# A second level of seven products in the gate and up products, and a deadline scheduler for units 2 to 27

## The chip, the core and the metric

The kernel runs on one core of a Trainium2 chip. The engines of that core are TensorE (PE, matrix products; its weight loads are shown as PEld), VectorE (DVE), ScalarE (ACT), GpSimd (POOL) and SyncE (SP); here POOL and SP only start DMA transfers, POOL those that add into DRAM or park a tile there, SP the plain loads and stores. Every engine works through its own instructions in the order in which the program lists them. The metric is the device time of one execution in microseconds (us), as a median over runs.

## What is computed

With x of 2048 rows and 512 columns, in fp32:

```python
xn = layernorm(x)                                # over the 512 columns
a, b = xn @ Wd_re.T, xn @ Wd_im.T                # DFT matrices, 512 x 512
A = Ws_re @ a - Ws_im @ b                        # DFT matrices, 2048 x 2048
g, u = xn @ w_gate, xn @ w_up                    # 512 x 1792 each
B = (gelu_tanh(g) * u) @ w_down                  # 1792 x 512
return x + A + B
```

## The kernel before

**Arithmetic.** An fp32 operand is split into a high part (`split_hi`, a copy on ACT that rounds to fp32r) and a low part (`split_lo`, a subtraction on DVE). `mm3` then makes one product of three matmuls: high by high, and high by low both ways. A matmul has 128 x 128 weights and 512 columns. All large products are done by a form of Strassen's algorithm with seven block products for a 2 x 2 block product (Winograd's form, with operands numbered 0 to 6), whose results are combined by copies between PSUM banks and by additions on DVE.

**Stages.** From 5 to 379.5 us the Fourier part runs (tiles `z`, `m`, `y`); its first two chunks are ordered by the planner below. From 379.5 to 771.3 us follow 28 units, and then the last down products.

**A unit.** `unit(n)` makes one 256-wide piece of the gate projection (n even) or of the up projection (n odd), for one half of the sequence: units 0 to 13 the first half, 14 to 27 the second (`NP` = 14; n // NP is the half `sp`). The weights are the same in both halves, unit n + 14 reads those of unit n again. A unit has seven products r, each over two blocks of 128 rows, so six matmuls each, in the order 0, 4, 5, 1, 6, 3, 2, in three PSUM banks `a`, `b`, `c`. Product 0 is the first: its result goes to bank `a` and is copied by ACT into bank `b` (line 1137), so that products 1 and 5, 6, 3 add to it in each. ACT copies `b` to the tile `q6` after product 5 and to `w` after product 6; DVE adds `c` to them. The four results go through gelu on ACT (`gate`, n even) or are multiplied in on DVE (`up_1`, n odd). Between the products stand "fills" (`fill`, up to four places per unit): pieces of the down product of earlier pairs (`down`), or, at first, the last Fourier products (`late_y`). The copies of a down product are added into DRAM (`partial`) by POOL's accumulating transfers.

**The work beside it.** `background(n)` lists, by hand, the DVE and ACT work of unit n: splits of the next unit's weights, sums of the weights of the unit after it (`weight_sums`), the same for the down weights `("d", q)`, the sums and splits of the hidden values of the pair before (`h_sum`, `h_split`), and the operands of x for the second half (`sums_xT`, `xT_split`), four of the seven of which are parked in DRAM (`PARKED`) and fetched again in units 11 to 13 (`FETCH`). `run(share)` issues a share of that list after certain products. `load_w(n + 2)` and `load_wd` start the weight loads one to two units ahead. In units 20, 21, 23 and 24 DVE finishes the output of the first half (`ends`, `finish`).

**Memory.** All tiles come from a pool of 109 slots of 128 x 512 (`SLOTS`); PSUM has eight banks.

**The planner.** `Plan` (line 37) is a list scheduler that runs when the program is built. `add` gives it an operation with its engine ("p" PE, "v" DVE, "a" ACT, "s" SP, "g" POOL), its price, what it comes after, which slots it makes and uses, and which banks. PE's operations stay in the order in which they are added. `deadlines` gives each PE operation the time at which it starts if PE never waits, and each other one the latest time that keeps those. `choose` picks the next operation on each engine: the earliest possible one, or one due sooner; it keeps the count of slots under a cap, starts an SP operation no sooner than `ahead` before it is due, and limits the transfers in flight. `run` then emits everything in the order found. Its prices are 0.6 us for a DVE and 0.52 for an ACT instruction of 512 columns (`V5`, `A5`) and 512/2400 + 0.0133 for a matmul (`MM`). Before the change it orders the first stage only, not the units.

**The tail.** `last_down` starts its first two banks in unit 27 and then works off the down products of the last two pairs.

Of the kernel before, what the change touches and what calls it, by code (L numbers as in the profile page):

```python
# [8 lines left out]
F32 = mybir.dt.float32  # L9
F32R = mybir.dt.float32r  # L10
# [4 lines left out]
P = 128  # L15
# [21 lines left out]
class Plan:  # L37
# [3 lines left out]
    LATE = 1e9  # L41
    LAND = .7

    def __init__(self, clocks, live, cap, ahead):
        self.clock, self.live, self.cap, self.ahead = dict(clocks), live, cap, ahead
        self.ops, self.users, self.ends, self.size = {}, {}, {}, {}
        self.products = None
        self.dma, self.flying = 0., {"s": [], "g": []}
        self.held, self.idle = {}, []
# [1 line left out]
    def done(self, name, at):  # L51
        self.ends[name] = at

    def add(self, name, engine, cost, fn, after=(), makes=(), uses=(), due=None, mb=0, banks=(), holds=(), adds=False):
        after = list(after)
        if engine == "p":
            if self.products:
                after.append(self.products)
            self.products = name
        self.ops[name] = dict(e=engine, cost=cost, fn=fn, after=after, makes=dict(makes), due=due, mb=mb, adds=adds, banks=tuple(banks), drains=bool(holds) and engine != "p")  # L60
        self.size.update(makes)
        for k in (*dict(makes), *uses):
            self.users.setdefault(k, set()).add(name)
        for k in (*banks, *holds):
            self.held.setdefault(k, set()).add(name)

    def deadlines(self):
        then = {n: [] for n in self.ops}
        for n, o in self.ops.items():
            for a in o["after"]:  # L70
                if a in self.ops:
                    then[a].append(n)
        t = self.clock["p"]
        for o in self.ops.values():
            if o["e"] == "p":
                o["due"], t = t, t + o["cost"]
        order, seen = [], set()

        def visit(n):
            stack = [(n, iter(then[n]))]  # L80
            seen.add(n)
            while stack:
                m, it = stack[-1]
                for c in it:
                    if c not in seen:
                        seen.add(c)
                        stack.append((c, iter(then[c])))
                        break
                else:
                    stack.pop()  # L90
                    order.append(m)
        for n in self.ops:
            if n not in seen:
                visit(n)
        for n in order:
            o = self.ops[n]
            own = self.LATE if o["due"] is None else o["due"]
            if o["due"] is None and o["drains"]:
                own = max([self.ops[a]["due"] + self.ops[a]["cost"] for a in o["after"] if a in self.ops and self.ops[a]["e"] == "p"],
                          default=self.LATE) + 4  # L100
            took = o["cost"] + (3.5 + o["mb"] * 2.6 if o["mb"] else 0)
            tail = self.TAIL[o["e"]]
            o["due"] = min([own] + [self.ops[c]["due"] - took - tail * (self.ops[c]["e"] != "p" or o["e"] != "p") for c in then[n]])
# [4 lines left out]
    def choose(self, ready, frees, spare):  # L108
        best = None
        for e, names in ready.items():  # L110
            able = []
            for n, at in names.items():
                o = self.ops[n]
                at = max(at, self.clock[e])
                if e == "s":
                    at = max(at, o["due"] - self.ahead)
                if o["mb"]:
                    k, room = self.parts(o), 8 if e == "s" else 7
                    for when, u in reversed(self.flying[e]):
                        k += u  # L120
                        if k > room:
                            at = max(at, when)
                            break
                if o["banks"]:
                    if len(self.idle) < len(o["banks"]):
                        continue
                    at = max([at] + self.idle[:len(o["banks"])])
                need = sum(o["makes"].values())
                if need:
                    cap = self.cap - (0 if o["due"] - at < 6 or not spare else 8 if e != "s" else 14)  # L130
                    live = self.live
                    for when, k in frees:
                        if when <= at:
                            live -= k
                        elif live + need > cap:
                            live -= k
                            at = when
                    if live + need > cap:
                        continue
                able.append((round(at, 1), o["due"], at, n))  # L140
            if not able:
                continue
            mine = min(able, key=lambda a: a[:2])
            until = mine[2] + self.ops[mine[3]]["cost"]
            for a in sorted(able, key=lambda a: a[1]):
                if a[2] < until - .1 and a[1] < min(mine[1] - 1, until):
                    mine = a
                    break
            if best is None or mine[2] < best[0]:
                best = mine[2], e, mine[3]  # L150
        return best

    def run(self):
# [3 lines left out]
        for n, o in self.ops.items():  # L157
            for a in o["after"]:
                if a in self.ops:
                    then[a].append(n)  # L160
        left = {k: len(u) + (len(u) == 1) for k, u in self.users.items()}
        of = {n: [] for n in self.ops}
        holding = {n: [] for n in self.ops}
        for k, u in self.held.items():
            for n in u:
                holding[n].append(k)
# [52 lines left out]
def fnet_geglu_kernel(ctx: ExitStack, tc: tile.TileContext, x, xt, cs, dh, wgu, wd, out):  # L219
# [16 lines left out]
    def slot(name, dtype=F32, shape=(P, D)):  # L236
        return mem.tile(list(shape), dtype, name=name, tag="mem")
# [4 lines left out]
    def hl_tile(name):  # L242

        return slot(name + "h", F32R), slot(name + "l", F32R)

    def hl_half(name):

        t = slot(name, F32R, (P, 2, HD))
        return t[:, 0], t[:, 1]

    def split_hi(t, src, sign=1):
        nc.scalar.activation(t[0], src, AF.Copy, scale=float(sign))  # L252
# [12 lines left out]
    def mm3(ps, a, sl, b, first, last, resumed=False, part=slice(3), late=0):  # L265

        for r, (u, v) in list(enumerate(((0, 0), (late, 1 - late), (1 - late, late))))[part]:
            nc.tensor.matmul(ps, a[u][:, sl], b[v], start=first and r == 0, stop=last and r == 2,  # L268
                             skip_group_check=resumed)
# [17 lines left out]
    def cols(j):  # L287
        return slice(j * P, (j + 1) * P)
# [9 lines left out]
    xnt = dram.tile([2, ND, P, CH], F32, name="xnt")  # L298
    d_park = dram.tile([7, 2, 2, P, 2, HD], F32, name="d_park")
    z_park = dram.tile([NC // 2, 2, 2, 2, P, CH], F32, name="z_park")  # L300


    xs, ln, xn = {}, {}, {}
# [377 lines left out]
    def flush():  # L681
        while pend:
            split_lo(*pend.pop(0))
# [158 lines left out]

    def weight_split(n, k):

        if k == 3:
            wl[n, 3] = hl_half("w")
            return wl[n, 3], wx[n][3][:, 0]
# [13 lines left out]
    def load_wd(q):  # L861

        if q < NP:
            wx["d", q] = [slot("wd", F32, (P, 2, HD)) for _ in range(2)]
            for i in range(2):
                nc.sync.dma_start(wx["d", q][i].rearrange("p a b -> p (a b)"), wd[q % (NP // 2), i])

    def product(n, k, ps, first=False):
        for i in range(2):
# [216 lines left out]
    def unit(n):  # L1086
# [48 lines left out]
        multiply(0, a, True)  # L1135
        q6, w = slot("q6"), slot("w")
        nc.scalar.activation(b, a, AF.Copy)
        multiply(4, c, True)
        while carry:
            carry.pop(0)()  # L1140
# [617 lines left out]
                y_out(c // 2, 3)  # L1758


    flush()
    add_w(1)
    carry.append(lambda: y_out(1, 6))
    for d in range(2):
        norm_xT(1, 0, d)
    last = last_down([NP - 2, NP - 1])
    for n in range(2 * NP):
        unit(n)
    for j in range(2):
        load_acc(1, 4, j)  # L1770
    for item in items:
        item()()
    next(last, None)


# [34 lines left out]
```

## Time and profile before

| | |
|---|---|
| median of 3 runs | 796.99 us (796.53 to 798.0) |
| the profiled execution | 796.45 us |
| its span | 794.7 us |
| PE busy, share of the span | 789.6 us, 99% |
| DVE, ACT, POOL busy | 718.9, 514.3, 162.0 us |
| moved by DMA | 179.58 MB |
| granted TensorE clock | 0.999 |

How to read it: a group of instructions is a line with the source line, the engine, the operation, output and inputs by the names of the tiles, count, busy time and mean length. Instructions of one engine overlap at their ends, so the mean length of one is longer than the distance between the starts of two. A chain piece or a timeline piece begins with its start and its length in us. The stretches list, for a window from one time to another, the busy us of PE, PEld, DVE, ACT and POOL, then PE's granted clock, the share of the DMA engines' time and GB/s. In this profile unit 0 begins at 379.54 us, unit 2 at 404.05, unit 4 at 431.34, unit 6 at 457.18, unit 14 at 571.42, unit 20 at 657.10, unit 26 at 742.78, and the tail at 771.34.

### The profile page before, as it was taken

What the parts mean: (1) busy time and instruction counts of PE and PEld (TensorE: products, weight loads), DVE (VectorE), ACT (ScalarE), POOL (GpSimd) and SP (SyncE); (2) the same over time, 40 slices, a digit from 0 to 9 for tenths busy, and PEclk for the clock granted to TensorE, in tenths of its full rate; (3) what the DMA queues carried; (4) which work ended last, traced back from release to release, by engine and by line L of the source; (5) the groups of instructions that cost most, each with busy time, mean ns of one, the idle gap of its engine ahead of it and who ended that gap; (6) DMA issues with size and microseconds to landing.
All of it is one profiled execution on the core that took longest, in us unless ns stands there. A gap on an engine that the chain in (4) does not pass through costs nothing.

```text
span 794.7 us, 11494 instructions
## 1 busy us (share of the span) xinstructions
PE 789.6 (99%) x3483; PEld 651.5 (82%) x3483; DVE 718.9 (90%) x1321; ACT 514.3 (65%) x982; POOL 162.0 (20%) x234
## 2 busy tenths in 40 slices
PE   9999999999999999999999999999999999999997
PEld 6888888888888888888888888888888888888886
DVE  7999999989999989899999998888878779989787
ACT  7997656547444655366667866766667676576663
POOL 0110420034211231000103422321222233122100
PEclk9999999999999999999999999999999999999999
DMA  9967997869999898779717977858975799887942
GB/s 340 364 174 228 344 350 258 269 242 243 365 372 363 296 304 292 254 263 308 169 55 162 218 144 164 203 90 213 263 142 86 124 252 140 181 203 140 256 95 106
DMA packets 94639, 179.58 MB, mean 226 GB/s; under 512 B 10960, under 2 KB 18672, under 8 KB 94384
## 3 DMA queue, kind: packets, MB, share of 16 engines
q1 hardware_dynamic: 68688, 118.80, 44.8%
q0 software_dynamic: 25600, 59.78, 35.4%
q8 instruction: 27, 0.44, 0.2%
q14 instruction: 36, 0.29, 0.1%
q10 hardware_dynamic: 288, 0.26, 0.1%
HBM read 116.13 MB, written 65.81 MB: 229 GB/s over the span
## 4 chain that ended last, share of the span: by engine, by line
PE 99%; DMA 0%; DVE 0%; ACT 0%; issue 0%
PE m L268 35%; PE dn L268 17%; PE b L268 14%; PE c L268 10%; PE y L268 10%; PE a L268 10%; PE z L268 4%; DMA x<-in_x 0%; DVE bn L332 0%; DVE p L1005 0%; DVE xa L355 0%; ACT w L343 0%; DVE stats L334 0%; PE st L1631 0%
## 5 line engine op out<-in xcount | busy, mean ns | idle before, releaser
L252 ACT ACTIVATE psh<-pan 128x512 fp32r<-128x512 f32 x203 | 115.6, 625 | 73.7 <-DVE pan L647 27.2
L257 DVE TENSOR_TENSOR psl<-pan,psh 128x512 fp32r<-128x512 f32 x198 | 128.5, 691 | 4.7 <-ACT psh L252 4.0
L926 POOL DMA_DIRECT2D partial<-part x94 | 80.8, 869 | 234.5 <-ACT part L925 200.3
L268 PE MATMUL m<-psh,xch 128*128 128x512 f32 x232 | 90.2, 389 | 0.0
L268 PE MATMUL m<-psl,xch 128*128 128x512 f32 x232 | 90.2, 389 | 0.0
L268 PE MATMUL m<-psh,xcl 128*128 128x512 f32 x232 | 90.2, 389 | 0.0
L925 ACT ACTIVATE part<-dn 128x512 f32<-128x512 f32 x94 | 55.4, 604 | 24.7 <-PE dn L268 22.4
L257 DVE TENSOR_TENSOR wl<-ws,wh 128x512 fp32r<-128x512 f32 x84 | 55.2, 685 | 0.1
L268 PEld LDWEIGHTS m<-psl,xch 128*128 128x128 f32 x232 | 43.5, 188 | 9.1
L268 PEld LDWEIGHTS m<-psh,xcl 128*128 128x128 f32 x232 | 43.5, 188 | 9.1
L268 PEld LDWEIGHTS m<-psh,xch 128*128 128x128 f32 x232 | 43.6, 188 | 9.0
L252 ACT ACTIVATE wh<-ws 128x512 fp32r<-128x512 f32 x84 | 49.6, 628 | 0.1
L1150 ACT ACTIVATE w<-b 128x512 f32<-128x512 f32 x28 | 16.7, 598 | 47.0 <-PE b L268 46.9
L568 POOL DMA_DIRECT2D partial<-part x28 | 20.9, 786 | 109.8 <-ACT part L564 104.0
L1153 DVE TENSOR_TENSOR w<-c,w 128x512 f32<-128x512 f32 x28 | 19.3, 690 | 24.5 <-ACT w L1150 24.5
L268 PE MATMUL m<-psh,xa 128*128 128x512 f32 x116 | 40.4, 389 | 0.0
L640 DVE TENSOR_TENSOR pan<-pan 128x512 f32<-128x512 f32 x58 | 38.2, 688 | 2.0 <-DMA pan<-in_cs 2.0
L257 DVE TENSOR_TENSOR htl<-s,hth 128x512 fp32r<-128x512 f32 x56 | 36.1, 688 | 4.2 <-ACT hth L252 4.1
L898 DVE TENSOR_TENSOR s<-s 128x512 f32<-128x512 f32 x56 | 37.5, 689 | 1.0
L257 DVE TENSOR_TENSOR wl<-wx,wh 128x512 fp32r<-128x512 f32 x28 | 19.2, 687 | 15.8 <-ACT wh L252 15.8
L252 ACT ACTIVATE hth<-s 128x512 fp32r<-128x512 f32 x56 | 32.4, 641 | 1.0 <-DVE s L898 1.0
L252 ACT ACTIVATE hh<-s 128x512 fp32r<-128x512 f32 x42 | 26.7, 635 | 9.4 <-DVE s L885 8.2
(774 smaller groups left out, 2338.6 us busy)
## 6 DMA issues: line engine op xcount, KB each, us to landing
pan<-in_cs SPq DMA_DIRECT2D x157, 256.0 KB, 5.4
partial<-part POOLq DMA_DIRECT2D x122, 256.0 KB, 5.4
wx<-in_wgu SPq DMA_DIRECT2D x56, 256.0 KB, 5.0
t_park<-pan POOLq DMA_DIRECT2D x29, 256.0 KB, 5.5
pan<-t_park SPq DMA_DIRECT2D x29, 256.0 KB, 4.8
wd<-in_wd SPq DMA_DIRECT2D x28, 256.0 KB, 4.3
acc<-partial SPq DMA_DIRECT2D x28, 256.0 KB, 5.8
zr<-z_park SPq DMA_DIRECT2D x16, 256.0 KB, 4.3
```

The lines of the kernel that those rows point to most:

```text
L252: nc.scalar.activation(t[0], src, AF.Copy, scale=float(sign))
L257: engine.tensor_sub(t[1], src, hi)
L268: nc.tensor.matmul(ps, a[u][:, sl], b[v], start=first and r == 0, stop=last and r == 2, skip_group_check=resumed)
L568: nc.gpsimd.dma_start(partial[sp, r, j], ypart.pop((r, j)), **({} if r in (0, 5, 6) else {"accum_op": OP.add}))
L640: return [lambda: nc.vector.tensor_sub(t3, b22, b12), lambda: nc.vector.tensor_sub(t1, b12, b11), lambda: (nc.vector.tensor_sub(b22, *((t1 ...
L898: nc.vector.tensor_sub(t, u, v)
L925: nc.scalar.activation(t, ps[j], AF.Copy)
L926: nc.gpsimd.dma_start(partial[sp, r, j], t, accum_op=OP.add)
L1150: nc.scalar.activation(w, b, AF.Copy)
L1153: nc.vector.tensor_add(w, c, w)
```

## The change

Two things change together.

First, units 2 to 27 are no longer run by `unit`. A new function `middle` gives all their work to a `Plan`: products in a written order, and everything on DVE, ACT, SP and POOL (weight loads, sums and splits, operands of x, copies out of banks, hidden values, down products with their accumulating transfers, the finishing of the first half, the loads of the last accumulators) by deadlines. `Plan` gets an argument `early`: an operation that makes tiles isn't started more than 16 us before it is due (`EARLY`), one that takes a bank not more than 3 us before; what has no deadline of its own is due just before PE's end. SP may load up to 16 us ahead (`FETCH_AHEAD`). Units 0 and 1 still run by hand.

Second, for the pairs of units 4 and 5, 6 and 7, to 12 and 13, product 0 is itself done by seven products, over the two units, the two row blocks and the two halves of the sequence (`inner_p`, `inner`). Each has one row block, so three matmuls. The operands of x for it are made once (`inner_x`), those of the weights once per pair (`inner_w`). The two results for the first half stay in PSUM: one in bank `a` of the even unit, one in bank `b2`, which serves as bank `a` of the odd unit. The two for the second half are parked in DRAM (`m_park`) and loaded again (`load_m`); units 18 to 27 (`fetched`) copy them into banks `b` and `a` in place of product 0, and need only half of their first weight split. The residual sums of x move to units 6 and 7 at the earliest, the x block (0, 1) is no longer parked and is split early, since the inner products use it.

Core of the diff:

```diff
+    LEAD = 4
+
+    def lead(n):
+        return n % 2 == 0 and LEAD <= n < NP
+
+    def fetched(n):
+        return isinstance(n, int) and n >= NP + LEAD
...
+    def inner(n, k, ps, first=False):
+
+        if k in (0, 1):
+            a, b = [t[:, cols(k)] for t in wl[n, 0]], xT[0, 0, k]
+        elif k == 3:
+            a, b = [t[:, cols(1)] for t in wl[n + 1, 0]], xi["hl", 3]
+        else:
+            a, b = [t[:, {4: 0, 5: 1, 6: 2, 2: 3}[k]] for t in wi["hl", n]], xi["hl", k] if k != 2 else xT[1, 0, 1]
+        mm3(ps, a, slice(P), b, first, True, resumed=not first)
...
+    U0, U1 = 2, 2 * NP
+    EARLY = 16
+    FETCH_AHEAD = 16
+    PARK = [(0, 0), *((k, i) for k in (1, 4, 5) for i in range(2))]
+
+    def middle():
+
+        plan = Plan(dict(p=.3, v=6.6, a=4.2, s=0., g=0.), 84, SLOTS - 2, FETCH_AHEAD, EARLY)
...
+        for n in range(LEAD, NP, 2):
+            for k in range(4):
+                add(("si", n, k), "v", .2, lambda n=n, k=k: inner_w(n, k), after=[("si", n, k - 1)] if k else [("lw", n), ("lw", n + 1)],
+                    uses=[("wx", n), ("wx", n + 1)] + [("wi", n)] * (k > 0), makes={} if k else {("wi", n): 1})
+            split_of(("iw", n), lambda n=n: inner_wsplit(n), [("si", n, 3)], [("wi", n)], {("wih", n): 2})
+            for j in range(2):
+                m = n + NP + j
+                add(("lm", m), "s", .45, lambda m=m: load_m(m), after=[("mp", m - NP)], mb=MB, makes={("m0", m): 1})
...
+            if lead(n):
+                b2, c2 = ("b2", n), ("c2", n)
+                inner_p(n, 0)
+                copy("ib", n, "b2", lambda n=n: bank_of(n, "a"), [("i", n, 0)], banks=[b2], holds=[a])
+                mult(n, 4)
+                inner_p(n, 1)
+                copy("sb", n, "b", lambda n=n: bank_of(n, "a"), [("i", n, 1)], banks=[b], holds=[a])
+            elif lead(n - 1):
+                copy("sb", n, "b", lambda n=n: bank[n - 1, "b2"], [("i", n - 1, 3)], banks=[b], holds=[a])
+                mult(n, 4)
+                inner_p(n - 1, 2)
+                sums("iaq", n - 1, "q2", "c2", [("i", n - 1, 2), ("iq", n - 1)], ("c2", n - 1))
+                add(("mp", n - 1), "g", .6, lambda n=n: nc.gpsimd.dma_start(m_park[n - 1], side[n - 1, "q2"]), after=[("iaq", n - 1)],
+                    uses=[("q2", n - 1)], mb=MB)
+            elif fetched(n):
+                copy("sb", n, "b", lambda n=n: m0[n], [("lm", n)], banks=[b], uses=[("m0", n)])
+                copy("sa", n, "a", lambda n=n: m0[n], [("lm", n)], banks=[a], uses=[("m0", n)])
+                mult(n, 4)
+            else:
+                mult(n, 0)
+                copy("sb", n, "b", lambda n=n: bank_of(n, "a"), [("p", n, 0)], banks=[b], holds=[a])
+                mult(n, 4)
+            d(0)
+            mult(n, 5)
+            copy("q6", n, "q6", lambda n=n: bank[n, "b"], [("p", n, 5)], holds=[b])
+            mult(n, 1)
+            hidden(n, (0, 0), [("p", n, 1)], lambda n=n: bank_of(n, "a"), [a], [])
+            d(1)
+            if lead(n):
+                inner_p(n, 4)
+            mult(n, 6)
...
+            if lead(n):
+                inner_p(n, 5)
+                copy("iq", n, "q2", lambda n=n: bank[n, "b2"], [("i", n, 5)], holds=[b2])
+            d(2)
+            mult(n, 3)
...
+            if lead(n):
+                inner_p(n, 6)
+                copy("iw", n, "w2", lambda n=n: bank[n, "b2"], [("i", n, 6)], holds=[b2])
+                sums("iaw", n, "w2", "c2", [("iw", n), ("i", n, 4)], c2)
...
+            d(3)
+            mult(n, 2)
...
+            if lead(n):
+                inner_p(n, 3)
...
     last = last_down([NP - 2, NP - 1])
-    for n in range(2 * NP):
+    for n in range(U0):
         unit(n)
-    for j in range(2):
-        load_acc(1, 4, j)
-    for item in items:
-        item()()
+    middle()
     next(last, None)
```

Here `mult(n, r)` is a product r of unit n, `inner_p(n, k)` an inner product k, `d(i)` the place of a fill, `copy` a copy on ACT and `sums` an addition on DVE.

More of the change, by code (lines that the diff above doesn't have):

```diff
@@ L42, with __init__ @@
     LAND = .7
-    def __init__(self, clocks, live, cap, ahead):
+    def __init__(self, clocks, live, cap, ahead, early=LATE):
+        self.early, self.had = early, set()
         self.clock, self.live, self.cap, self.ahead = dict(clocks), live, cap, ahead
@@ L52, in done, with add @@
         self.ends[name] = at
-    def add(self, name, engine, cost, fn, after=(), makes=(), uses=(), due=None, mb=0, banks=(), holds=(), adds=False):
+    def add(self, name, engine, cost, fn, after=(), makes=(), uses=(), due=None, mb=0, banks=(), holds=(), adds=False, begin=0.):
         after = list(after)
@@ L59, in add @@
             self.products = name
-        self.ops[name] = dict(e=engine, cost=cost, fn=fn, after=after, makes=dict(makes), due=due, mb=mb, adds=adds, banks=tuple(banks), drains=bool(holds) and engine != "p")
+        self.ops[name] = dict(e=engine, cost=cost, fn=fn, after=after, makes=dict(makes), due=due, mb=mb, adds=adds, begin=begin, banks=tuple(banks), drains=bool(holds) and engine != "p")
         self.size.update(makes)
@@ L76, in deadlines @@
                 o["due"], t = t, t + o["cost"]
+        late = self.LATE if self.early == self.LATE else t - 1
         order, seen = [], set()
@@ L96, in deadlines @@
             o = self.ops[n]
-            own = self.LATE if o["due"] is None else o["due"]
+            own = late if o["due"] is None else o["due"]
             if o["due"] is None and o["drains"]:
                 own = max([self.ops[a]["due"] + self.ops[a]["cost"] for a in o["after"] if a in self.ops and self.ops[a]["e"] == "p"],
-                          default=self.LATE) + 4
+                          default=late) + 4
             took = o["cost"] + (3.5 + o["mb"] * 2.6 if o["mb"] else 0)
@@ L113, in choose @@
                 o = self.ops[n]
-                at = max(at, self.clock[e])
+                at = max(at, self.clock[e], o["begin"])
                 if e == "s":
                     at = max(at, o["due"] - self.ahead)
+                elif o["makes"] and not o["begin"]:
+                    at = max(at, o["due"] - self.early)
                 if o["mb"]:
@@ L124, in choose @@
                 if o["banks"]:
+                    if e != "p":
+                        at = max(at, o["due"] - 3)
                     if len(self.idle) < len(o["banks"]):
@@ L129, in choose @@
                 if need:
[L130 to L138, printed above, removed]
+                    found = None
+                    for then in (at, max(at, o["due"] - 6)):
+                        cap = self.cap - (0 if o["due"] - then <= 6 or not spare else 8 if e != "s" else 14)
+                        live = self.live
+                        for when, k in frees:
+                            if when <= then:
+                                live -= k
+                            elif live + need > cap:
+                                live -= k
+                                then = when
+                        if live + need <= cap and (found is None or then < found):
+                            found = then
+                    if found is None:
                         continue
+                    at = found
                 able.append((round(at, 1), o["due"], at, n))
@@ L160, in run @@
                     then[a].append(n)
-        left = {k: len(u) + (len(u) == 1) for k, u in self.users.items()}
+        left = {k: len(u) + (len(u) == 1 and k not in self.had) for k, u in self.users.items()}
         of = {n: [] for n in self.ops}
@@ L165, in run @@
             for n in u:
-                holding[n].append(k)
+                if n in holding:
+                    holding[n].append(k)
         held, last = {k: len(u) for k, u in self.held.items()}, {}
@@ L300, in fnet_geglu_kernel @@
     z_park = dram.tile([NC // 2, 2, 2, 2, P, CH], F32, name="z_park")
+    m_park = dram.tile([NP, P, CH], F32, name="m_park")
     xs, ln, xn = {}, {}, {}
@@ L843, in weight_split @@
     def weight_split(n, k):
-        if k == 3:
-            wl[n, 3] = hl_half("w")
-            return wl[n, 3], wx[n][3][:, 0]
+        if k == 3 or (k == 0 and fetched(n)):
+            p, src = (3, wx[n][3][:, 0]) if k else (1, wx[n][0][:, 1])
+            wl[n, p] = hl_half("w")
+            return wl[n, p], src
         v = slot("wh", F32R, (P, 2, HD)), slot("wl", F32R, (P, 2, HD))
@@ L866, in load_wd, with inner_x, inner_xsplit, inner_w @@
                 nc.sync.dma_start(wx["d", q][i].rearrange("p a b -> p (a b)"), wd[q % (NP // 2), i])
+    LEAD = 4
[3 more added lines that the diff above has]
+        return isinstance(n, int) and n >= NP + LEAD
+    m0, xi, wi = {}, {}, {}
+    def inner_x(k):
+        b11, b21 = (xr[0, i, 0] for i in range(2))
+        b12, b22 = (xr[1, i, 0] for i in range(2))
+        u, v = {6: (b22, b12), 4: (b12, b11), 5: (b22, xi.get(4)), 3: (b21, xi.get(5))}[k]
+        xi[k] = slot("xi")
+        nc.vector.tensor_sub(xi[k], u, v)
+    def inner_xsplit(k):
+        xi["hl", k] = hl_tile(f"xi{k}")
+        return xi["hl", k], xi[k]
+    def inner_w(n, k):
+        a, b = (wx[m][0][:, 0] for m in (n, n + 1))
+        if k == 0:
+            wi[n] = slot("wi", F32, (P, 4, P))
+        op, u, v = ((OP.add, b[:, :P], b[:, P:]), (OP.subtract, wi[n][:, 0], a[:, :P]), (OP.subtract, a[:, :P], b[:, :P]),
+                    (OP.subtract, a[:, P:], wi[n][:, 1]))[k]
+        nc.vector.tensor_tensor(wi[n][:, k], u, v, op=op)
+    def inner_wsplit(n):
+        wi["hl", n] = slot("wih", F32R, (P, 4, P)), slot("wil", F32R, (P, 4, P))
+        return wi["hl", n], wi.pop(n)
+    def inner(n, k, ps, first=False):
[6 more added lines that the diff above has]
+        mm3(ps, a, slice(P), b, first, True, resumed=not first)
     def product(n, k, ps, first=False):
@@ L1134, in unit @@
         a, b, c = ps_tile("a"), ps_tile("b"), ps_tile("c")
-        multiply(0, a, True)
         q6, w = slot("q6"), slot("w")
-        nc.scalar.activation(b, a, AF.Copy)
+        if fetched(n):
+            for t in (b, a):
+                nc.scalar.activation(t, m0[n], AF.Copy)
+        else:
+            multiply(0, a, True)
+            nc.scalar.activation(b, a, AF.Copy)
         multiply(4, c, True)
```

265 lines of the change are left out of this document (added).

## The prediction

> **What bounds the kernel now.** I read the page's summary first, then who TensorE (PE) waited for, then the chain that ended last, and only then the stretches of the stage that the change rewrites. The page:
>
> ```profile
> span 794.7 us, 11494 instructions
> PE 789.6 (99%) x3483; PEld 651.5 (82%) x3483; DVE 718.9 (90%) x1321; ACT 514.3 (65%) x982; POOL 162.0 (20%) x234
> ...
> PE 99%; DMA 0%; DVE 0%; ACT 0%; issue 0%
> ...
> L268 PE MATMUL m<-psh,xch 128*128 128x512 f32 x232 | 90.2, 389 | 0.0
> ```
>
> PE is busy for all but 5.1 us and carries 99% of the closing chain. The waits of PE are the whole list of what another engine made it wait for by the groups of waits:
>
> ```profile
> PE warm L1211 <- PEq L1803: 0.8, 1, 0.8
> PE z L268 <- DVE xa L355: 0.2, 1, 0.2
> ```
>
> Both lie at the start. The chain's last pieces show the pitch of one product and the tail:
>
> ```profile
> 757.74 1.36 PE a L268 x6
> ...
> 771.34 19.24 PE dn L268 x90
> 790.58 0.02 issue
> 790.60 0.42 DVE p L1005
> ```
>
> Six matmuls take 1.36 us, so one of 512 columns costs 0.2267 us. The 389 ns that the groups give as a mean is one matmul's length with its overlap, and is no price. So time leaves this kernel only if a matmul leaves it, and any wait put before PE is paid in full. The rewritten stage is units 2 to 27, 404.05 to 771.34. Its tight stretches are units 2 to 5, units 6 to 13 and units 20 to 25 (columns: busy us of PE, PEld, DVE, ACT, POOL; granted clock; DMA share; GB/s):
>
> ```profile
> 404.05:457.18 53.13, 53.13 (x235) 43.84 (x235) 52.09 (x99) 39.57 (x78) 17.39 (x23) 1.00 0.71 156
> 457.18:571.42 114.24, 114.24 (x505) 94.59 (x505) 99.64 (x188) 79.90 (x155) 28.98 (x37) 1.00 0.80 181
> 657.10:742.78 85.68, 85.68 (x379) 70.95 (x379) 76.55 (x145) 57.03 (x112) 21.11 (x25) 1.00 0.85 176
> ```
>
> PE has no gap, VectorE (DVE) is filled to 98%, 87% and 89%, ScalarE (ACT) to 74%, 70% and 67%.
>
> **The matmuls.** For a pair of units n, n+1 the first product costs 6 matmuls per unit and half of the sequence: 4 x 6 = 24. The new form has seven products of one 128-row block each, three matmuls apiece: 21, all spent in the first half. Pairs 4, 6, 8, 10 and 12 do it: 5 x 3 = 15 matmuls fewer, 15 x 0.2267 = 3.40 us. By halves: units 4 to 13 get 5 x 9 = 45 more, units 18 to 27 get 10 x 6 = 60 fewer.
>
> The Trainium skill, "TensorE: Matmul & The Clock Gate", section "Wait — 56ns, not 53.3ns?", puts a warm matmul of 512 columns at 215.7 ns; by that 15 would give an estimated 3.24 us. The row above says 226.7 ns for these fp32r products, and the measurement decides.
>
> **What is paid beside PE.** Prices are the distance from start to start, since an instruction's end overlaps the next one's start:
>
> ```profile
> 407.28 0.68 DVE L257 TENSOR_TENSOR hl<-s,hh 128x512 fp32r<-128x512 f32 x1
> 407.88 0.68 DVE L1169 TENSOR_TENSOR q<-c,q 128x512 f32<-128x512 f32 x1
> ...
> 410.21 0.42 DVE L834 TENSOR_TENSOR ws<-wx 128x256 f32<-128x256 f32 x1
> 410.55 0.42 DVE L834 TENSOR_TENSOR ws<-wx,ws 128x256 f32<-128x256 f32 x1
> ```
>
> ```profile
> 410.02 0.62 ACT L252 ACTIVATE wh<-wx 128x512 fp32r<-128x512 f32 x1
> 410.54 0.62 ACT L252 ACTIVATE wh<-ws 128x512 fp32r<-128x512 f32 x1
> ...
> 415.57 0.43 ACT L252 ACTIVATE w<-wx 128x256 fp32r<-128x256 f32 x1
> 415.88 1.68 ACT L252 ACTIVATE hth<-s 128x512 fp32r<-128x512 f32 x3
> ```
>
> DVE: 0.60 us at 512 columns, 0.34 at 256; a 128-column one is 0.21 by the same slope (an estimate). ACT: 0.52 and 0.31.
>
> Once, for units 2 to 4: four sums of x blocks and four splits, 8 x 0.60 = 4.8 us of DVE, 4 x 0.52 = 2.1 of ACT. Per pair: four weight sums (0.84) and their low half (0.60), two sums out of the banks (1.20): 2.64 of DVE; one high half and three copies: 2.1 of ACT. Per fetched unit in the second half: one more copy (+0.52 ACT), and a weight split of half the width (-0.26 DVE, -0.21 ACT). The residual sums of x (six of 0.60) move from units 4 and 5 to 6 and 7 at the earliest.
>
> Units 2 to 5: DVE 52.09 + 4.8 + 2.64 + 1.44 (the next pair's weights) - 3.6 = 57.4, while PE's room grows by 9 matmuls to 55.2. That is 2.2 us too much, unless it goes later. It can: the sums and splits of hidden pair 1 (8 x 0.60), done in unit 4, feed down products whose turn comes from unit 6 on, and the parked x splits (0,0) and (1) wait for unit 14. Units 6 to 13 then carry 99.6 + 4 x 2.64 - 1.44 + 3.6 + 2.2 = 114.5 in a room of 114.2 + 8.2 = 122.4, so 94%. Units 20 to 25: 76.6 - 1.6 = 75.0 in 85.68 - 6 x 1.36 = 77.5, so 97%. ACT comes to 44.3 of 55.2 and 58.9 of 77.5. So the work fits beside PE in every stretch, but in two of them with little to spare: cost taken 0, upper bound the 2.2.
>
> **The new chains of copies.** In a lead unit the bank copy ahead of product 5 follows the second inner product, with one fill of 6 matmuls, 1.36 us, as cover; before, another product stood there too, 2.72. What such a copy needs:
>
> ```profile
> 762.79 0.39 PE L268 MATMUL b<-xT51h,wl 128*128 128x512 f32 x1
> ...
> 763.22 0.60 ACT L1145 ACTIVATE q<-b 128x512 f32<-128x512 f32 x1 [2.73 <-PE b L268]
> ```
>
> ```profile
> 772.27 0.19 PEld L268 LDWEIGHTS dn<-hl,wh 128*128 128x128 f32 x1 [0.23 <-DVE hl L257]
> ```
>
> From the start of the last matmul to the copy's end are 1.03 us, less the matmul's own 0.23 that is 0.80; 0.05 for the way back to PE. So 0.5 us is left: one other ACT instruction (0.52) may stand in front, two (1.04) make PE late by 0.5. Behind the waiting copy in ACT's order stand the high halves of weights, which PE needs a unit later. The other new copies (after inner products 5 and 6) have 2.72 and 1.36 us too, and the last inner product of a lead unit needs the low half of unit n+1's weights a unit earlier than before, which DVE's order has to give. The rows bound it: 0 below, since a copy can't make PE run ahead of its 1.36; above, 0.5 in each of 5 lead units at two places, 5 us. I take 0, nearer to the rows of ACT (74% full), and keep half the upper end for a rival. Two more banks are held across a pair; the only short bank or operand wait in the trace is the 0.23 above, so at most 10 x 0.23 = 2.3, taken as 0.
>
> **DMA and queues.** 10 parked partial sums on POOL and 10 loads of them on SP are new; one x block, two parks and two loads of the parked kind, is no longer parked. The costs and the stretches where they fall:
>
> ```profile
> wx<-in_wgu SPq DMA_DIRECT2D x56, 256.0 KB, 5.0
> acc<-partial SPq DMA_DIRECT2D x28, 256.0 KB, 5.8
> ...
> q1 hardware_dynamic: 68688, 118.80, 44.8%
> ```
>
> ```profile
> 431.34:444.94 13.60, 13.60 (x61) 11.26 (x61) 13.14 (x25) 10.36 (x21) 6.55 (x9) 1.00 1.06 261
> 444.94:457.18 12.24, 12.24 (x55) 10.14 (x55) 12.14 (x25) 10.84 (x22) 5.08 (x6) 1.00 1.01 177
> ```
>
> 118.8 MB take 0.448 x 794.7 = 356 us of the engines, so 256 KB take 0.79. Units 20 to 25 get 6 loads, 4.7 us on 0.85 x 85.7 = 72.8: 77.5 of 77.5, full. Units 4 and 5 were full already (1.06, 1.01) with PE at 13.60 of 13.60, because their loads are issued a unit ahead; the planner issues up to 16 us ahead, three times the 5.0 to landing. Taken as 0. POOL was busy 17.39 of 53.13 us there, and ten issues more hide in it; nothing waits for the park itself until the other half of the sequence. The loads of the last accumulators, now set by the planner too, have the same cover; without it each is worth its 5.8.
>
> **The order itself.** Nearly every DVE, ACT, SP and POOL instruction of units 2 to 27 gets a new place. What can be shown of such orders is the first stage, planned by the same class:
>
> ```profile
> 38.00:85.60 47.60, 47.60 (x212) 39.40 (x211) 47.18 (x100) 39.88 (x83) 8.60 (x13) 1.00 0.74 223
> 85.60:172.80 87.20, 87.20 (x387) 72.10 (x386) 83.79 (x146) 49.97 (x87) 19.14 (x35) 1.00 0.87 294
> ```
>
> DVE at 99% and 96%, ACT at 84% and 57%, and no gap on PE; and the planner's prices (0.6 and 0.52 us, 512/2400 + 0.0133 a matmul) are the distances read above. Taken as 0. A gain is excluded: the one wait of PE after its start that could go is the 0.23 in the tail.
>
> **Sum.** The profiled execution took 796.45 us, 1.75 outside its span, and lies 0.54 under the median of the three runs, 796.99. 796.45 - 3.40 = 793.05 for such an execution, 793.6 for the median: 0.43% faster. About 0.2%, 1.6 us, is what a measurement of this kernel tells from no change.
>
> **The rivals.**
> - The fill of DVE or ACT shows a little. If the 2.2 us of units 2 to 5 isn't put off, because an order by deadlines takes parked x work first, PE waits for it: 795.8. If two copies in five lead units come late by 0.5 each at half the places, 2.5: 796.1. For it: DVE at 98% in units 2 to 5 before anything is added, and 97% in 20 to 25. Against: the deferrable work is larger than the excess, and the first stage ran at 99%. It gives between 795.4 and 798.6, no measurable change.
> - Slower: tiles run out, and a load comes late. The inner operands hold eight tiles from unit 3 to 13, and a pair some six more; the planner may then issue a weight or parked load only shortly before its use. One exposed load costs 5.0 from issue to landing and 0.52 + 0.60 for its split: 6.1, so 793.6 + 6.1 = 799.7; two give 805.8. It decides from 5.0 us of PE waits on (3.4 gained and 1.6 beyond). For it: full DMA in units 4 and 5 and, worked out, in 20 to 25, and 16 us of allowed lead are worth nothing when no tile is free. Against: no PE wait of before is a load's, in stretches as full.
> - That the change doesn't save what it says is no separate case: the 15 matmuls are counted in the code, and each new one has the shape of those whose pitch was read above, 128x128 by 512.
>
> The Trainium skill, same page, section "HAM oscillation — how this bites in real kernels", warns of PE idle gaps above about 3.4 us, after which the clock is halved. By it the exposed load would cost an estimated 1.7 us more (half of one such window), 801.4. No gap of that kind is in this trace, whose granted clock is 1.00 in the whole stage.
>
> **How the numbers follow.** Forecast, no gap worth naming: 0.61, and its own range is 792.9 (the lowest run, 796.53, less 3.40 and the 0.23) to 795.4. Little shows: 0.14. Slower: 0.25; of that about half is one exposed load, half more. The range from 792.9 to 801.0 takes in the first two, and one exposed load, and leaves out some 0.13 above and little below. Faster 0.61, same 0.14, slower 0.25.
>
> **What would show it.** PE at 3468 matmuls, its busy time down by 3.4 to about 786.2; the chain still 99% PE and no PE wait above 0.3 in the middle stage; DVE's share up to about 97% until unit 9; the six-matmul pitch unchanged. Wrong would be: PE waits on the weights' low halves in units 4 to 9 (DVE's excess), on copies L1137's successors make in lead units, on a load of a parked sum or of weights in units 12 to 25 with DMA near 1.0, or a longer tail than 794.7 - 771.34 = 23.4 us because a last accumulator comes late.

## The result, and the profile after

| | before | changed |
|---|---|---|
| median of 7 runs each, us | 796.9 (796.53 to 798.0) | 794.38 (794.31 to 794.83) |
| ratio, 95% interval | | 0.9967 (0.9956 to 0.9979) |
| the profiled execution and its span, us | 796.45, 794.7 | 794.38, 792.6 |

The change makes the kernel faster by 0.33%, with an interval from 0.21% to 0.44%. Of the forecast 3.4 us some 2.5 came. The experiments below ran on three chips, on which the kernel of before took 797.15, 798.18 and 796.77 us as a median (single executions 796.59 to 799.44), so each of their ratios is to before on the same chip. The page's first lines and its chain, of the changed kernel:

```profile
span 792.6 us, 11549 instructions
PE 787.7 (99%) x3468; PEld 648.7 (82%) x3468; DVE 731.9 (92%) x1364; ACT 534.4 (67%) x1016; POOL 168.2 (21%) x242
...
PE 90%; DVE 6%; DMA 1%; ACT 1%; issue 1%; ACTq 0%; DVEq 0%
```

There are 15 matmuls fewer, 3468. But the chain is no longer 99% PE: for 10% of the span it runs over DVE, ACT and transfers, because it leaves PE at one wait, at 416.32 us, and comes back to PE far earlier. So PE waited at least there. The groups of waits name it, beside the wait at the start:

```profile
PE warm L1274 <- PEq L2232: 0.8, 1, 0.8
PE b L280 <- ACT w L1993: 0.3, 1, 0.3
```

The timeline of PE shows more than the 0.3 us (start, length, engine, line, operands). These are the places in units 1 and 2 where two starts lie more than 0.3 us apart, and the first product of unit 3:

```profile
402.79 0.39 PE L280 MATMUL b<-xT31h,w 128*128 128x512 f32 x1
403.18 0.50 PE L280 MATMUL c<-xT20h,wh 128*128 128x512 f32 x1
403.52 0.40 PE L280 MATMUL c<-xT20l,wh 128*128 128x512 f32 x1
...
412.65 0.39 PE L280 MATMUL y<-t311l,dh 128*128 128x512 f32 x1
413.00 0.50 PE L280 MATMUL b<-xT60h,wh 128*128 128x512 f32 x1
413.33 0.39 PE L280 MATMUL b<-xT60l,wh 128*128 128x512 f32 x1
...
415.64 0.39 PE L280 MATMUL y<-t301l,dh 128*128 128x512 f32 x1
416.32 0.50 PE L280 MATMUL b<-xT30h,w 128*128 128x512 f32 x1 [0.29 <-ACT w L1993]
416.66 0.40 PE L280 MATMUL b<-xT30l,w 128*128 128x512 f32 x1
...
419.21 0.39 PE L280 MATMUL a<-xT00h,wh 128*128 128x512 f32 x1
```

From 402.79 to 419.21 lie 67 matmuls, 15.19 us at 0.2267; they took 16.42. So 1.23 us were lost, 0.31 at the end of unit 1, which is still ordered by hand, and 0.92 in unit 2, the first that the planner orders. From unit 3 on to the tail no two starts lie apart by more than they should: all units with inner products and all that fetch their parked sums run without a gap, and the pitch in them is that of before:

```profile
452.69 4.08 PE b L280 x18
...
769.57 19.29 PE dn L280 x90
```

The stretches that answer to the three shown of before (units 2 to 5, 6 to 13, 20 to 25):

```profile
404.65:460.85 56.20, 55.91 (x245) 45.61 (x245) 50.88 (x101) 40.10 (x76) 17.07 (x23) 1.00 0.65 133
460.85:583.25 122.40, 122.40 (x542) 101.35 (x541) 112.77 (x219) 91.67 (x175) 34.12 (x46) 1.00 0.78 179
666.20:743.70 77.50, 77.50 (x344) 64.17 (x343) 72.06 (x139) 59.25 (x117) 17.29 (x20) 1.00 0.87 217
```

The reader is to see PE's 122.40 of 122.40 and 77.50 of 77.50, and DVE at 91%, 92% and 93%. Busy time hides part of a loss: the first row shows 0.29 us without a matmul, the starts in it a loss of 0.92.

**Where the 2.1 us between the two profiled spans come from.** 15 matmuls give 3.40; the seam of units 1 and 2 takes 1.23, where before lost about 0.1 between the same two products. Two more lie outside the stage that the change rewrites, and cancel. The first product of the kernel started at 5.38 us instead of 5.03, after a load of x that took 2.79 us instead of 2.43. And the last store, issued at 789.34, ended the span 3.3 us later; before, issued at 791.05, it ended it 3.65 later. Whether these two are chance, one profile of before can't say. The last store of the changed kernel:

```profile
789.34 0.33 SPq L1065 DMA_DIRECT2D out_y<-p  x1
```

Some 0.2 us are left over, 0.1 of them in a gap in unit 0 (383.84 us) that before doesn't have.

### The profile page after: what moved, and what is told of

It is laid out like the page before. It is cut to its first block, busy times and chain, and to the rows that moved or that the text cites. A ratio compares the mean times of both kernels' runs of the same rounds, so it can differ in the third digit from the quotient of the medians.

```text
span 792.6 us, 11549 instructions
## 1 busy us (share of the span) xinstructions
PE 787.7 (99%) x3468; PEld 648.7 (82%) x3468; DVE 731.9 (92%) x1364; ACT 534.4 (67%) x1016; POOL 168.2 (21%) x242
## 4 chain that ended last, share of the span: by engine, by line
PE 90%; DVE 6%; DMA 1%; ACT 1%; issue 1%; ACTq 0%; DVEq 0%
PE m L280 33%; PE dn L280 17%; PE b L280 15%; PE c L280 10%; PE y L280 6%; PE a L280 5%; PE z L280 4%; DVE wl L269 1%; DVE ws L847 1%; DVE xr L780 1%; DMA dl<-d_park 1%; DMA wd<-in_wd 0%; DVE xr L781 0%; DMA x<-in_x 0%; DVE psl L269 0%
## 5 line engine op out<-in xcount | busy, mean ns | idle before, releaser
L2034 ACT ACTIVATE part<-dn 128x512 f32<-128x512 f32 x94 | 55.2, 597 | 35.6 <-PE dn L280 33.1
L280 PE MATMUL dn<-hl,wh 128*128 128x512 f32 x84 | 32.8, 390 | 0.0
L280 PE MATMUL dn<-hh,wh 128*128 128x512 f32 x84 | 32.7, 389 | 0.0
L280 PE MATMUL dn<-hth,wh 128*128 128x512 f32 x84 | 32.7, 389 | 0.0
L280 PE MATMUL dn<-hth,wl 128*128 128x512 f32 x84 | 32.7, 389 | 0.0
```

Of the source, the lines that this page charges most:

```text
L2034: nc.scalar.activation(part[0], tiles[j], AF.Copy)
```

## Experiments

The theory after the result: the gain is the matmuls alone; the order gains nothing and loses at the seam (the step from the units ordered by hand to those of the planner), because the planner starts from a picture of unit 2's beginning that isn't true. On ACT in the changed kernel:

```profile
407.53 0.61 ACT L264 ACTIVATE wh<-wx 128x512 fp32r<-128x512 f32 x1
411.15 1.30 ACT L264 ACTIVATE wh<-ws 128x512 fp32r<-128x512 f32 x2 [3.01 <-DVE ws L847]
412.36 0.58 ACT L1993 ACTIVATE q<-b 128x512 f32<-128x512 f32 x1
...
414.14 0.63 ACT L264 ACTIVATE xT01h<-xr 128x512 fp32r<-128x512 f32 x1
414.66 0.63 ACT L264 ACTIVATE xT00h<-xr 128x512 fp32r<-128x512 f32 x1
415.18 0.59 ACT L577 ACTIVATE part<-y 128x512 f32<-128x512 f32 x1
415.66 0.60 ACT L1993 ACTIVATE w<-b 128x512 f32<-128x512 f32 x1
```

ACT stands idle 3.0 us before a high half of unit 3's weights whose sums (`ws`) DVE hasn't made yet, and the copy `q6`, for which PE's product 6 waits, is behind it in the order. The backlog then makes the copy `w` late for product 3. In the code the reason is plain: the sums of unit 3's weights are made by unit 1's background work, so they are no operation of the new plan, and whatever isn't in the plan counts as ready at zero (`plan.ends.setdefault(a, 0.)`).

**Telling the planner the truth about the seam.**

```diff
-        plan = Plan(dict(p=.3, v=6.6, a=4.2, s=0., g=0.), 84, SLOTS - 2, FETCH_AHEAD, EARLY)
+        plan = Plan(dict(p=.3, v=7.7, a=4.2, s=0., g=0.), 84, SLOTS - 2, FETCH_AHEAD, EARLY)
         plan.idle = [0.] * 5 + [1., 1.5, 2.]
+        plan.done(("sw", U0 + 1, 3), 7.7)
```

> The planner of units 2 to 27 is told that the sums of unit 3's weights are ready only at 7.7 us after its zero, and that VectorE is busy with unit 1's work until then (6.6 before); nothing else changes. Theory: the two PE gaps of unit 2 (0.24 and 0.62 us) come from ScalarE's order, where the high halves of unit 3's weights stand before the copies that PE needs and wait 3.0 us for sums that the planner takes as ready at zero. Then both gaps go, some 0.85 us, and the time is about 793.5. Rival: the copies are late because VectorE and ScalarE have too much to do there; then a truer start changes nothing, 794.4, or moves the gaps.

Measured: 793.43 us, 0.9957 of before (0.9945 to 0.997). ACT's order is now another, the copies stand where PE needs them:

```profile
410.51 0.60 ACT L1994 ACTIVATE q<-b 128x512 f32<-128x512 f32 x1 [0.94 <-PE b L280]
411.00 0.62 ACT L264 ACTIVATE wh<-wx 128x512 fp32r<-128x512 f32 x1
411.52 0.62 ACT L264 ACTIVATE wh<-ws 128x512 fp32r<-128x512 f32 x1
...
414.64 0.60 ACT L1994 ACTIVATE w<-b 128x512 f32<-128x512 f32 x1 [0.30 <-PE b L280]
```

Both copies wait for PE instead of PE for them. The 67 matmuls took 15.48 us instead of 16.42, and the only PE wait left in the groups is that at the start. The theory's 0.85 us are there, the rival falls. Unit 1 still lost 0.29.

**Half of that edit:** only the line with `plan.done`, at 6.6.

> Half of the edit that took the gaps of unit 2 away: the planner is told that the sums of unit 3's weights are ready at 6.6 us, VectorE's start stays as it was. Theory (the missing readiness of these sums alone puts the high halves ahead of the copies): both gaps gone, as with the whole edit, about 0.85 us under the changed kernel. Rival (VectorE's start, 1.1 us too early, is what misplaces the copies): the gaps stay.

Measured: 793.56 us, 0.9958 (0.9946 to 0.9971), no gap in unit 2. The missing readiness of the sums alone did it. The changed kernel run again on this chip:

> The changed kernel as it is, beside the other two on the same chip: 0.3% faster than before again, gaps of 0.3, 0.24 and 0.6 us in units 1 and 2.

Measured: 794.34 us, 0.9967 (0.9955 to 0.998), with the same three gaps. The intervals of the two ratios overlap, as before scatters, but the executions don't: 793.51 to 793.80 with `plan.done`, 794.06 to 794.70 without.

**The scheduler without the second level.**

```diff
-    LEAD = 4
+    LEAD = NP
-    PARK = [(0, 0), *((k, i) for k in (1, 4, 5) for i in range(2))]
+    PARK = [(k, i) for k in (0, 1, 4, 5) for i in range(2)]
```

(and the inner operands of x are not made.)

> Units 2 to 27 by the deadline scheduler, but no inner products, so the matmuls of before. Theory (PE's matmuls set the time, the order only what is lost at the seam): 0 saved, 0.3 to 1.2 us lost in units 1 and 2, so 797.0 to 798.1, that is no gain over 796.9. Rival (the order itself brings the gain): below 796.

Measured: 797.32 us, 1.0002 of before (0.9993 to 1.0011), with the gaps of unit 2 and the same name in the waits. The new order by itself gains nothing. Whether the second level would run without gaps under an order by hand was not tried. Unit 1 lost only 0.01 us here.

**Three pairs instead of five.**

```diff
-    LEAD = 4
+    LEAD = 8
```

> Inner products from unit 8 on instead of unit 4: three pairs, 9 matmuls fewer instead of 15. Theory: 9 x 0.2267 = 2.04 us saved, the seam's loss as before, so 1.36 us more than the changed kernel, about 795.7. If the inner operands made in units 2 to 4 were what is late at the seam, the loss of 0.85 would go and it would be about 794.9.

Measured: 794.93 us, 0.9973 (0.9965 to 0.9982), 0.8 less than the theory and near the other number. The trace decides otherwise: the gaps of units 1 and 2 are there in full (0.45 us again ahead of product 3 in unit 2), and from the last of unit 1's products 3 to the last matmul it took 386.94 us, 1.16 more than the changed kernel's 385.78, where six matmuls are 1.36. What made the whole time shorter lies after the last matmul, where the last store ended the span 2.80 us after its issue, against 3.3 in the changed kernel's two profiles. So the dose is right within 0.2 us between these matmuls. Why the last store landed sooner is open, and a difference of half a microsecond between two medians need not come from the middle units.

**The first stage in the order of before.** The edits of `choose` act on the first stage's plan too; I had overlooked that. The instruction orders differ there mainly in two families, the sums and splits of x and the operands of the 512 x 512 DFT. Here the first stage has the old rule:

```diff
+class FirstPlan(Plan):
+
+    def choose(self, ready, frees, spare):
...
-    plan = Plan(dict(p=10.9, v=12.0, a=11.7, s=5.6, g=8.0), 18, SLOTS - 2, AHEAD)
+    plan = FirstPlan(dict(p=10.9, v=12.0, a=11.7, s=5.6, g=8.0), 18, SLOTS - 2, AHEAD)
```

> The changed kernel, with the choice rule of before kept for the first stage, whose order the edits in the planner have moved too. Theory: the gap of 0.31 us in unit 1, which is still ordered by hand, comes from VectorE arriving 0.4 us later there after a differently ordered first stage; then 0.3 less, about 794.1. Rival: VectorE's lag comes from where tiles and loads fall later on; then 794.4 and the same gap.

Measured: 794.21 us, 0.9969 (0.9956 to 0.9981). Unit 1's gap shrank from 0.31 to about 0.15 us, and the 67 matmuls took 16.21. The effect on the time is inside the interval. Both edits together:

> The seam told rightly, and the first stage chosen by the rule of before. Theory: the two effects add, 0.85 from unit 2 and 0.15 to 0.3 from unit 1 (its gap shrank from 0.31 to 0.15 us in the run with the first stage as before), so 0.1 to 0.3 us under the seam's run; rival: unit 1's gap is chance and it stays level with that run.

Measured: 793.35 us, 0.9954 (0.994 to 0.9967); the 67 matmuls took 15.37, 0.18 over their pitch. The time is level with the seam's run. Its five executions spread from 793.05 to 794.35; the profiled one is the slowest, and its PE lost some 0.8 us in the Fourier part, at 245 to 249 us. The first stage's order is not by itself what makes unit 1 late: the run with the scheduler alone has the first stage of the changed kernel, and unit 1 lost 0.01 us in it. What makes it late is open. In the changed kernel the added lag of DVE, 0.4 us, first appears at 338.9 us, where a high half of a panel came later than before, in a stage ordered by hand.

**More work for VectorE.** If DVE's fill is what these units are near to, useless sums must cost time:

```diff
             sums("aw", n, "w", "c", [("w", n), ("p", n, 4)], c)
+            for i in range(1 if LEAD <= n < NP else 0):
+                add(("idle", n, i), "v", V5, lambda n=n: nc.vector.tensor_add(junk, side[n, "w"], side[n, "w"]), after=[("aw", n)], uses=[("w", n)],
+                    due=unit_at(n) + 14)
```

> One useless VectorE sum of 512 columns more in each of units 4 to 13, 10 x 0.6 = 6 us in a stretch where VectorE is busy 112.8 of 122.4 us in the changed kernel. Theory (an order by deadlines fills VectorE up to nearly the whole stretch): 118.8 of 122.4, no PE wait in these units, 794.4. Rival (at 92% every further VectorE instruction is late for PE): up to 6 us more, 800.

Measured: 794.59 us, 0.996 (0.9945 to 0.9976). With `range(2 ...)`:

> Two such sums per unit, 12 us: 124.8 of 122.4 us. Theory: the excess of 2.4 us has to show, partly as PE waits in units 6 to 13 and partly as work put off to the units after 13, so 794.4 to 797. If VectorE isn't what these units are near to, it stays at 794.4.

Measured: 794.56 us, 0.9956 (0.9941 to 0.997). Units 6 to 13 with two more sums:

```profile
460.85:583.25 122.40, 122.40 (x541) 101.35 (x540) 121.04 (x234) 91.71 (x174) 33.42 (x44) 1.00 0.80 180
```

The stretch behind them, in the changed kernel and then with two more sums:

```profile
583.25:612.00 28.75, 28.75 (x129) 23.80 (x128) 26.26 (x50) 19.18 (x37) 6.85 (x8) 1.00 0.75 148
583.25:612.00 28.75, 28.75 (x128) 23.81 (x127) 27.52 (x52) 19.55 (x37) 6.92 (x8) 1.00 0.76 142
```

In units 6 to 13 VectorE is busy 121.04 of 122.40 us, 99%, and PE has no gap. From the last of unit 1's products 3 to the last matmul the two runs took 385.79 and 385.81 us, the changed kernel 385.78. The excess that I had reckoned with shows in the second of the two forms expected, as work put off. All sixteen sums lie in these units, but VectorE has only fifteen instructions more there, 234 instead of 219 and 121.04 us instead of 112.77: two others have come in from units ahead, and three (low halves of a hidden value, of an x operand and of a weight) have moved behind unit 13, where it is busy 27.52 us instead of 26.26. PE waits for none of it. That the fifteen add 0.55 us each and not 0.60 is left open. So in units 4 to 13 the time of VectorE is not what this kernel is near to; a further sum that PE itself needs was not tried.

**Eight tiles fewer for the planner.**

```diff
-        plan = Plan(dict(p=.3, v=6.6, a=4.2, s=0., g=0.), 84, SLOTS - 2, FETCH_AHEAD, EARLY)
+        plan = Plan(dict(p=.3, v=6.6, a=4.2, s=0., g=0.), 84, SLOTS - 10, FETCH_AHEAD, EARLY)
```

> The changed kernel with eight tiles fewer for the planner of units 2 to 27 (99 of 109 instead of 107). Theory (loads have lead to spare, the order finds room): the time stays within 1 us of 794.4, no PE wait on a load. Rival (tiles decide, loads come late when none is free): PE waits of some 5 to 6 us for each exposed load, so 800 or more.

Measured: 803.86 us, 1.008 of before (1.0059 to 1.0101). The waits of PE, and its timeline where a parked x operand is loaded late in unit 14 (`xT41h` was issued at 579.12 us, in the changed kernel at 566.60):

```profile
PE c L280 <- DMA xT41h<-xT_hl: 2.9, 1, 2.9
PE b L280 <- ACT w L1993: 2.3, 1, 2.3
PE c L280 <- DMA xT41l<-xT_hl: 1.2, 1, 1.2
```

```profile
584.31 0.39 PE L280 MATMUL c<-xT40h,wl 128*128 128x512 f32 x1
587.62 0.50 PE L280 MATMUL c<-xT41h,wh 128*128 128x512 f32 x1 [2.93 <-DMA xT41h<-xT_hl]
589.28 0.80 PE L280 MATMUL c<-xT41l,wh 128*128 128x512 f32 x1 [1.16 <-DMA xT41l<-xT_hl]
589.88 0.63 PE L280 MATMUL c<-xT41h,wl 128*128 128x512 f32 x1
590.30 0.63 PE L280 MATMUL dn<-hh,wh 128*128 128x512 f32 x1
590.73 0.63 PE L280 MATMUL dn<-hh,wl 128*128 128x512 f32 x1
```

The rival's mechanism is real, eight tiles away from the changed kernel: one operand without room, two loads, costs 4.5 us of gaps, then the matmuls run at a pitch of 0.43 us, some 2.8 us more, and a late copy adds 2.4. From the last of unit 1's products 3 to the last matmul it took 395.32 us, 9.5 more than the changed kernel.

**Loads at most 6 us ahead.**

```diff
-    FETCH_AHEAD = 16
+    FETCH_AHEAD = 6
```

> The planner may start SP's loads only 6 us before they are due instead of 16. Theory: the planner's own allowance for a load (5.2 us at 256 KB twice) lies inside the due time, so a load still lands in time unless the DMA engines are full; up to 1 us of PE waits where they are, 794.4 to 795.4. Rival (the 16 us of lead are what keeps loads in time): PE waits of several us each time the DMA engines are full, 797 or more.

Measured: 801.27 us, 1.0043 of before (1.003 to 1.0056), but not for the reason of either side. Units 3 to 27 have no gap. PE waits in the tail:

```profile
PE dn L280 <- DVE wl L269: 2.2, 2, 1.3
PE dn L280 <- DVE hl L269: 2.0, 1, 2.0
```

The weights of the last two down products have no product in the plan that needs them, so they are due only at its end. With little lead they were issued at 737.74 instead of 730.85, their splits stood in DVE's order at the tail's start, and the hidden values' low halves came behind them. This is read from the code and the trace; no run gave these loads a due time. In the middle 6 us of lead are enough.

## Why the prediction was right, and where a size was off

- **The matmuls, 3.40 us.** Right: 3468 of them, the pitch unchanged, no gain without the second level, and with three pairs the share of three.
- **DVE's fill.** The sums were close (114.5 worked out for units 6 to 13, 112.77 measured; 75.0 and 72.06 for units 20 to 25), and that the excess of units 2 to 5 would be put off is shown: 50.88 us in 56.20, not 57.4 in 55.2. The rival built on it falls for units 4 to 13 with the two runs of useless sums; units 20 to 25, at 93%, had no gap.
- **The new chains of copies, 0 to 5 us, taken as 0.** Right: no gap in any lead unit.
- **Banks, 0 to 2.3, and DMA, taken as 0.** Right. But the 0.23 in the tail was not the only short wait for an operand or a bank in the trace of before: its list of the waits of weight loads also has `PEld c L268 <- DVE w L1153: 0.2, 1, 0.2`, in unit 2. Units 20 to 25 showed a DMA share of 0.87, not the 1.0 that I worked out, and no wait.
- **The order itself, "taken as 0".** This is the term that was mis-sized. It measured 0.9 us of PE gaps in unit 2, which telling the planner of the sums took away; with unit 1's 0.3, whose cause stays open, the seam lost 1.23. The evidence that I took, a first stage planned without a gap, says that the planner's prices hold; it says nothing of the state from which a plan starts. The prediction named neither the seam nor the work left over from unit 1. The code had it: a predecessor outside the plan counts as done at zero. That the edits of the planner reorder the first stage too was also missed; its worth is not above the noise.
- **Slower by a late load.** Did not happen. The experiment with eight tiles fewer shows that tiles run short somewhere between the 107 of the changed kernel and 99, and that one late operand costs 7.3 us, 4.5 of gaps and some 2.8 of slow matmuls, where the prediction had 6.1. The Trainium skill, "TensorE: Matmul & The Clock Gate", section "HAM oscillation — how this bites in real kernels", which the prediction cited beside it, warns of PE gaps above about 3.4 us. The effect came, a halved clock, but after gaps of at most 3.1 us in this run and of at most 2.2 us in the run with later loads, so the measurement decides; the last section has the numbers.
- **What would show it.** PE's busy time fell to 787.7, not 786.2, the chain is 90% PE and not 99%, and the tail was no longer than before. "No PE wait above 0.3" was true to the letter by the groups of waits, and hid the loss: that view shows 0.3 where the starts show 1.23.

The version with the seam told rightly is faster than both kernels: 793.43 us, and 793.56 with half of the edit, against 794.34 to 794.38 for the changed one; on profiles it takes 0.94 us out of the 67 matmuls between units 1 and 3.

## What to carry to other kernels

Where one engine has no gaps, count its instructions: what leaves it is the gain, as long as the others keep up; here VectorE did with 99% of a stretch filled. When a scheduler takes over in the middle of a program, look at what it believes of the moment at which it starts; work left over from the part before, which isn't among its operations, is its blind spot, and one instruction that waits in an in-order queue makes everything behind it late. Read lost time of a saturated engine from the distance of the starts, not from the list of waits.

## What the runs showed of the hardware

After gaps PE's matmuls ran at half speed for some 5 us. With eight tiles fewer, 13 matmuls from 589.88 to 595.00 started 0.43 us apart instead of 0.23, and the granted clock of that stretch is 0.50; two gaps of 3.1 and 1.4 us lie right before, with one matmul between them. In the same run a single gap of 2.4 us, at 600.52, cost no clock: from the second on the matmuls after it came 0.23 to 0.24 apart. In the run with later loads the clock fell after gaps of 1.5, 1.0 and 2.2 us, none of them above the 3.4 us of the Trainium skill's section cited above; PE was busy 2.17 of 6.30 us there (columns: busy us of PE, PEld, DVE, ACT, POOL, then the granted clock, the share of the DMA engines' time and GB/s):

```profile
769.00:775.30 6.30, 2.17 (x9) 0.92 (x7) 6.30 (x13) 3.32 (x8) 0.00 (x0) 0.85 0.28 86
775.30:780.00 4.70, 4.70 (x11) 3.73 (x12) 4.60 (x8) 2.41 (x5) 0.00 (x0) 0.50 0.00 0
```

So here several gaps close together did what one gap of 2.4 us alone did not. Short single waits (those of the seam) cost no clock, but more than the wait itself: the first matmul after one lasts 0.50 instead of 0.39 us, and the next starts 0.33 or 0.34 after it instead of 0.23.
